# Batch 1's first stage behind batch 0's, the first decodes through PSUM, the last weights decoded earlier

## The chip, the cores and the metric

One core of a Trainium2 chip runs the kernel. The metric is the device time of one execution in microseconds (us), as the median of several. The core has four computing engines with queues of their own: TensorE (PE, with its weight loads as PEld), VectorE (DVE), ScalarE (ACT) and GpSimd (POOL). SyncE (SP) issues most of the DMAs here, and ACT some of the stores. Each queue is worked off in order, so an instruction that waits holds up all that stand behind it on its engine.

## The reference

Three stages follow each other. `x` of one is the result of the one before, 4608 rows of 512.

```
p_packed = softmax(p @ k.T / 8) @ v             # 8 batches x 8 heads, 32 packed rows of 64, 576 keys
out      = softmax(q @ p_packed.T / 8) @ p_packed
x        = out, heads side by side              # 4608 x 512
h = x @ w_in;  x = (h * sigmoid(h)) @ w_out     # 512 -> 2048 -> 512
a = x @ w1;  b = x @ w2                         # 512 -> 1024
out = ((a * b) @ w3) @ w_out2                   # 1024 -> 1024 -> 512
```

The weights come to the chip as 64-bit words and have to be decoded to 32-bit floats there. All products are done in three passes on a high and a low part of each operand (`mm3`: L96, L97, L98).

## The kernel before

**Slots.** The first two stages run as one list of 256 items (8 batches, 2 halves of 288 rows, 16 blocks `m` of 128 hidden columns), called slots here and numbered from 0. A slot has 18 matmuls of 288 columns on PE: six for `ps_h` (the hidden block) and, three slots later (`LAG` = 3), twelve for `ps_x` (its product with `w_out`). Between them stand `sg` (a tanh on ACT), `gg` (DVE, L795), `gh` (ACT) and `gl` (POOL, L89). `ps_h` has two banks, so the `ps_h` of a slot waits for the `gg` of two slots before. The lefthand operand `mq` of a slot is loaded (`mr`, a DMA), rounded by a DVE cast (L84) and completed by a POOL subtraction; two `mr` buffers exist.

**What is woven in.** Beside the slots run units: `Pack` (attention of the packed rows), `Spread` (attention of the queries), and `PackIn` (product of packed values and `w_in`, with `wi` and `ps_m`). Which one is handed out in which slots is set by `over` and `pack_in` (`paces`); a scheduler then orders the instructions of each engine by its own costs. The start is handed out by the string `START`: P0 and P1 are the packs of batches 0 and 1, S0 and S1 the two halves of the queries of batch 0, L a load of an encoded weight, F a decode, D and T products of batch 0 and 1 with `w_in`, W a store of a decoded weight; "|" ends a slot.

**Decoding.** One decode (`Decode`) of a 128x512 block is two operations on ACT (the high and the low words, in place in `raw`), a shift on DVE (L164, `z<-raw`), an addition on POOL (L165, `z<-z,raw`) and a combination on DVE (L166, `z<-raw,z`). The first 32 decodes, of `w_in` and `w_out`, stand in the first 56 slots.

**The last weights.** From slot 209 to slot 250, `prepare_second` prepares the third stage: 40 decodes of `wo2`, `w3`, `w1` and `w2`, the splits `wo`, `w3T`, sums and splits `w12s` on DVE and ACT, and 16 groups of 12 products of 512 columns, `ps_w` (w3 times `wo2`), into one bank, whose splits `w34s` are done by ACT and DVE.

**Third stage.** After slot 255 come 36 items of `ps_ab` and `ps_o` (L1086, L96 to L98), which the change leaves as they are.

Of the kernel before, what the change touches and what calls it, by code (L numbers as in the profile page):

```python
# [22 lines left out]
def attention_swiglu_chain(  # L23
# [109 lines left out]
    w34_d = [dram.tile([128, 2, 512], F32, name=f"w34_d{i}") for i in range(KM2)]  # L133
    x2_d = {(b, f): dram.tile([128, CD, HS], F32, name=f"x2_d{b}_{f}") for b in range(B) for f in range(2)}
# [7 lines left out]
    ps_acc = psum_a.enter_context(tc.tile_pool(name="ps_acc", bufs=4, space=PSUM))  # L142
    ps_h = psum_a.enter_context(tc.tile_pool(name="ps_h", bufs=2, space=PSUM))
    ps_f = psum_a.enter_context(tc.tile_pool(name="ps_f", bufs=2, space=PSUM))

# [4 lines left out]
    class Decode:  # L150
# [7 lines left out]
        def __init__(self, raw, z):  # L158
            def word(dtype, t):
                return raw.bitcast(dtype).rearrange("p (n t) -> p n t", t=2)[:, :, t]  # L160

            act_copy(word(F32, 1), word(F32, 1), 2.0**-112)
            act_copy(word(I32, 0), word(U32, 0), 2.0**-29)
            V.tensor_scalar(out=z, in0=word(I32, 1), scalar1=3, scalar2=None, op0=ALU.logical_shift_left)  # L164
            G.tensor_tensor(out=z, in0=z, in1=word(I32, 0), op=ALU.add)  # L165
            V.scalar_tensor_tensor(  # L166
                out=z, in0=word(I32, 1), scalar=-(2**31), in1=z, op0=ALU.bitwise_and, op1=ALU.bitwise_or
            )
            self.z = z.bitcast(F32)
# [5 lines left out]
    class Decodes:  # L175


        def __init__(self, srcs, finish, raw, room):
            self.srcs, self.finish, self.raw, self.room = srcs, finish, raw, room
            self.n = 0  # L180
            self.end = len(srcs)
            self.raws = []
# [7 lines left out]
        def step(self):  # L190
# [4 lines left out]
            self.finish(n, Decode(self.raws.pop(0), self.room(n)))  # L195
# [42 lines left out]
    class Lane:  # L238
# [99 lines left out]
    class Pack(Rows):  # L338
# [26 lines left out]

        def load_v(self):
            self.v = self.lane.v_rows()
            move(out=self.v, in_=v[self.b, self.hg])

        def split_v(self, f):  # L370
            if self.lane.plain:
                return
            if f == 0:
                self.vp = self.lane.parts([128, 4, 5, 64], "v")
            r, cs = self.PARTS[f]
            hi, lo, src = (x[0:r, :, cs] for x in (*self.vp, self.v))
# [7 lines left out]
        def steps(self):  # L384
# [34 lines left out]
            for c in range(5):  # L419
# [3 lines left out]
                    [x[0:r, c] for x in ep], [x[0:r, :, c] for x in self.vp], c == 0, c == 4,  # L423
# [208 lines left out]
    def direct(g, c):  # L632

        assert all(("i", CD * g + c) in ready for c in range(CD))
# [28 lines left out]
    def finish_fill(n, d):  # L663
# [10 lines left out]
        finish_fill, fill_raw, lambda n: zi[order[n][1]].bitcast(I32) if order[n][0] == "i" else at_room(n),  # L674
    )
# [72 lines left out]
    def fetch(u):  # L748

        while True:  # L750
# [16 lines left out]
            t = g_p.tile([128, 2, 128], F32, tag="mr", name="mr", bufs=2)  # L767
            src = source(b, g, j)
            n = 128 // len(src)
            for y, x in enumerate(src):  # L770
                move(out=t[n * y:n * y + n], in_=x)
            split_hi(slots[:, far, :, 0], t, True)
# [472 lines left out]
```

## Time and profile before

| | us |
|---|---|
| median of 3 runs | 1493.23 (1491.17 to 1495.48) |
| the profiled execution, device time | 1495.0 |
| its span, first to last instruction | 1493.2 |

Busy shares of the span: PE 94%, PEld 88%, DVE 63%, ACT 45%, POOL 40%. The profile's ends of matmuls are modelled, so PE counts as busy between matmuls that follow closely; how fast it really goes is read from how many matmuls stand in a stretch. A share over the whole span is a mean over stretches with different limits: the page's slices show PE below full in the first four and again about half way, where DVE is at nine tenths or more.

### The profile page before, as it was taken

The page shows a single profiled execution, that of the slowest core. Times are in us where ns is not written, and L with a number is a line of the kernel's source. Part 1 is how long each engine was busy: PE and PEld are TensorE (multiplying, and loading weights), DVE is VectorE, ACT ScalarE, POOL GpSimd, SP SyncE. Part 2 cuts the span into 40 slices and gives each one's busy share as a digit, 9 for nine tenths or more (in the row PEclk, how much of TensorE's full clock was granted, in tenths as well). Part 3 has the DMA queues.
Part 4 walks back from the last instruction along what each step waited for, and adds up shares of the span by engine and source line. Part 5 has one row for each costly group of instructions (what it writes and reads, how often), then busy time and mean ns, then how long its engine had stood idle before and what let it go on. Part 6 is the DMA issues. An engine that isn't in the chain of part 4 may idle for free.

```text
span 1493.2 us, 25861 instructions
## 1 busy us (share of the span) xinstructions
PE 1410.7 (94%) x9548; PEld 1318.6 (88%) x9548; DVE 935.8 (63%) x1743; ACT 665.7 (45%) x1442; POOL 596.0 (40%) x606
## 2 busy tenths in 40 slices
PE   6789999999999999999788889999999999999999
PEld 4577899899999999999777779899999999999998
DVE  6977757548674486646999995364553645536443
ACT  5766555645565455644455653132221323213221
POOL 4689645766678456674876552000000000000000
PEclk9989999999999999999999999999999999999999
DMA  7687533754466243542468778810100101101000
GB/s 253 233 295 246 157 96 106 214 147 126 118 184 171 75 121 95 160 112 83 157 216 268 244 238 295 344 57 1 57 29 29 57 1 57 29 29 58 1 29 29
DMA packets 139263, 194.77 MB, mean 130 GB/s; under 512 B 14464, under 2 KB 101504, under 8 KB 138112
## 3 DMA queue, kind: packets, MB, share of 16 engines
q1 hardware_dynamic: 123904, 178.43, 37.4%
q10 hardware_dynamic: 15232, 14.68, 3.0%
q8 instruction: 75, 1.23, 0.3%
q14 instruction: 52, 0.43, 0.1%
HBM read 133.76 MB, written 59.31 MB: 129 GB/s over the span
## 4 chain that ended last, share of the span: by engine, by line
PE 64%; DVE 15%; issue 6%; DMA 6%; ACT 4%; POOL 3%; SPq 1%; ACTq 0%; DVEq 0%; POOLq 0%
PE ps_ab L1086 24%; PE ps_o L96 5%; PE ps_o L97 5%; PE ps_o L98 5%; PE ps_x L96 5%; PE ps_x L98 5%; PE ps_x L97 5%; DMA mr<-m_d 3%; PE ps_h L96 2%; PE ps_h L97 2%; PE ps_h L98 2%; DVE z L166 2%; DVE w12s L89 2%; DVE z L164 1%; DVE mq L84 1%
## 5 line engine op out<-in xcount | busy, mean ns | idle before, releaser
L96 PE MATMUL ps_x<-gh,wo 128*128 128x288 f32 x1024 | 303.7, 300 | 5.0 <-DVE xs L824 2.4
L97 PE MATMUL ps_x<-gh,wo 128*128 128x288 f32 x1024 | 301.4, 298 | 0.0
L98 PE MATMUL ps_x<-gl,wo 128*128 128x288 f32 x1024 | 286.1, 299 | 4.2 <-POOL gl L89 3.9
L89 POOL TENSOR_TENSOR gl<-gg,gh 128x288 fp32r<-128x288 f32 x256 | 226.2, 889 | 106.6 <-ACT gh L80 91.8
L1086 PE MATMUL ps_ab<-xct,w 128*128 128x256 f32 x1728 | 221.4, 284 | 0.0
L1086 PEld LDWEIGHTS ps_ab<-xct,w 128*128 128x128 f32 x1728 | 215.1, 190 | 1.0
L96 PEld LDWEIGHTS ps_x<-gh,wo 128*128 128x128 f32 x1024 | 194.4, 190 | 10.2 <-DVE xs L824 4.1
L80 ACT ACTIVATE gh<-gg 128x288 fp32r<-128x288 f32 x256 | 112.6, 442 | 194.2 <-DVE gg L795 190.7
L97 PEld LDWEIGHTS ps_x<-gh,wo 128*128 128x128 f32 x1024 | 194.3, 190 | 2.2 <-issue 1.3
L98 PEld LDWEIGHTS ps_x<-gl,wo 128*128 128x128 f32 x1024 | 188.1, 190 | 7.4 <-POOL gl L89 5.6
L89 POOL TENSOR_TENSOR mq<-mr,mq 128x256 fp32r<-128x256 f32 x176 | 143.6, 816 | 121.0 <-DVE mq L84 110.0
L96 PE MATMUL ps_h<-a,mq 128*128 128x288 f32 x512 | 159.8, 312 | 33.9 <-DVE gg L795 30.2
L1086 PE MATMUL ps_ab<-xcb,w 128*128 128x256 f32 x1296 | 176.9, 283 | 2.8 <-DMA w<-w_d 2.8
L1103 DVE TENSOR_TENSOR r<-p,ps_ab 128x512 f32<-128x512 f32 x72 | 49.2, 684 | 205.6 <-PE ps_ab L1086 205.4
L1086 PEld LDWEIGHTS ps_ab<-xcb,w 128*128 128x128 f32 x1296 | 168.1, 189 | 7.3 <-issue 2.9
L97 PE MATMUL ps_h<-a,mq 128*128 128x288 f32 x512 | 154.7, 302 | 0.8 <-POOL mq L89 0.8
L98 PE MATMUL ps_h<-a,mq 128*128 128x288 f32 x512 | 153.5, 300 | 0.0
L84 DVE CAST mq<-mr 128x256 fp32r<-128x256 f32 x176 | 85.1, 484 | 103.5 <-PE ps_h L98 52.2
L795 DVE SCALAR_TENSOR_TENSOR gg<-sg,ps_h 128x288 f32<-128x288 f32 x256 | 113.9, 447 | 48.6 <-ACT sg L791 42.2
L96 PEld LDWEIGHTS ps_h<-a,mq 128*128 128x128 f32 x512 | 98.0, 191 | 48.4 <-DVE gg L795 41.6
L791 ACT ACTIVATE sg<-ps_h 128x288 f32<-128x288 f32 x256 | 101.9, 404 | 52.9 <-PE ps_h L98 46.6
L97 PE MATMUL ps_o<-w,abl 128*128 128x512 f32 x280 | 109.7, 392 | 0.0
(165 smaller groups left out, 2619.4 us busy)
## 6 DMA issues: line engine op xcount, KB each, us to landing
mr<-m_d SPq DMA_DIRECT2D x144, 128.0 KB, 2.6
raw<-in_moe_w_dram SPq DMA_DIRECT2D x32, 512.0 KB, 4.3
w_d<-w12s ACTq DMA_DIRECT2D x56, 256.0 KB, 3.0
w<-w_d SPq DMA_DIRECT2D x8, 1792.0 KB, 14.2
wz<-wi_d SPq DMA_DIRECT2D x48, 256.0 KB, 3.4
m_d<-ms SPq DMA_DIRECT2D x96, 128.0 KB, 2.8
raw<-in_moe_w_out_dram SPq DMA_DIRECT2D x21, 512.0 KB, 4.8
vr<-in_v_dram SPq DMA_DIRECT2D x16, 640.0 KB, 4.2
```

The lines of the kernel that those rows point to most:

```text
L80: A.activation(out=dst, in_=src, func=ACTF.Copy, scale=mul)
L84: V.tensor_copy(out=hi, in_=src)
L89: (eng or V).tensor_tensor(out=lo, in0=src, in1=hi.bitcast(F32), op=ALU.subtract)
L96: T.matmul(out=dst, lhsT=wh, rhs=xh, start=start, stop=False)
L97: T.matmul(out=dst, lhsT=wl, rhs=xh, start=False, stop=False)
L98: T.matmul(out=dst, lhsT=wh, rhs=xl, start=False, stop=stop)
L164: V.tensor_scalar(out=z, in0=word(I32, 1), scalar1=3, scalar2=None, op0=ALU.logical_shift_left)
L166: V.scalar_tensor_tensor(out=z, in0=word(I32, 1), scalar=-(2**31), in1=z, op0=ALU.bitwise_and, op1=ALU.bitwise_or)
L791: ins = A.activation(out=sg, in_=ps, func=ACTF.Tanh, scale=0.5)
L795: V.scalar_tensor_tensor(out=gg, in0=sg, scalar=1.0, in1=ps, op0=ALU.add, op1=ALU.mult)
L1086: T.matmul(out=bank[:, x], lhsT=w[:, wp], rhs=xt[:, kt, xp], start=first and (x, kt, n) == (0, 0, 0), stop=last and (x, kt, n) == (1, 1, 2 ...
L1103: V.tensor_tensor(out=dst, in0=p, in1=q, op=op)
```

## The change

1. `START` is written anew: the packs of batch 1 (P1) stand directly behind those of batch 0, before most decodes; S1 comes behind them, and products (T) and stores (W) are spread over more slots. P1 loads its values in pieces into buffers of decoded weights (`vz`).
2. As long as no accumulator of a slot is in use, a decode writes its high words to a PSUM bank (`ps_dec`). The two DVE operations then read PSUM, and POOL's addition comes last instead of between them.
3. The 40 late decodes leave `prepare_second`. They are handed out in slots 70 to 205 (pace "z"), their operations held behind the `sg` of their slot, loads behind an `mr` load; each result is stored to `late_d` in HBM from ACT's queue and is loaded again by `prepare_second` (12 buffers, up to six ahead).
4. `mr` has three buffers, and the split of an `mq` that is not needed in the next slot is handed out one slot after its load, behind a `gg`.

```diff
     START = (
-        "P0.load P0.load_v P0.split_v0 S0.load P0.prepare L L L L P0 F P0 F L P0 F "
...
+        "P0.load P0.load_v P0.split_v0 S0.load P0.prepare L L L P1.load P1.load_v P1.prepare P1.split_v0 L L "
+        "P0 P0 P0 P0 P0.tail S0 S0 P1 F L F L S1.load S0 P1 F L F L D D P1 F L F L P1 F L F L D D P1.tail F "
+        "| F F S1 | F S1 | F F S1 | F F | F F T T | F F T T | F W W | F T T W W | F F T T | W W T T "
...
+    late_d = [dram.tile([128, 512], F32, name=f"late_d{n}") for n in range(5 * KM2)]
...
-        def __init__(self, raw, z):
+        def __init__(self, raw, z, ps=None):
...
-            act_copy(word(F32, 1), word(F32, 1), 2.0**-112)
+            high = word(F32, 1) if ps is None else ps
+            act_copy(high, word(F32, 1), 2.0**-112)
             act_copy(word(I32, 0), word(U32, 0), 2.0**-29)
...
+            high = high.bitcast(I32)
+            V.tensor_scalar(out=z, in0=high, scalar1=3, scalar2=None, op0=ALU.logical_shift_left)
...
+            else:
+
+                V.scalar_tensor_tensor(
+                    out=word(I32, 0), in0=high, scalar=-(2**31), in1=word(I32, 0),
+                    op0=ALU.bitwise_and, op1=ALU.bitwise_or,
+                )
+                G.tensor_tensor(out=z, in0=z, in1=word(I32, 0), op=ALU.add)
...
+        lambda: None if acc else acc_bank(1, "ps_dec"),
...
+        while came and u:
+            with tc.issue_after(behind["gg"]):
+                parts(*came.pop(0))
...
-            t = g_p.tile([128, 2, 128], F32, tag="mr", name="mr", bufs=2)
+            t = g_p.tile([128, 2, 128], F32, tag="mr", name="mr", bufs=3)
...
+                behind["mr"] = move(out=t[n * y:n * y + n], in_=x).ins
+            if nxt > u + 1:
+                came.append((far, t))
+            else:
+                parts(far, t)
...
+        load()
+        load()
+        yield
+        for n in range(len(late)):
+            if n + 2 < len(late):
+                load()
+            with tc.issue_after(behind["sg"]):
+                z = Decode(raws[n], room(n)).z
+            store(out=late_d[n], in_=z, age=1)
+            yield
...
+            def load():
+                n = len(zs)
+                zs.append(dp.tile([128, 512], F32, tag="z", name="z", bufs=12))
+                move(out=zs[n], in_=late_d[n])
...
+    paces["z"].append((70, at0 + 13, len(late) + 1))
```

Here `at0` is 192, so the pace ends at slot 205.

**DVE at slot 228.** Three places show how the instructions move. The first is DVE's queue at slot 228, in the preparation of the third stage, as it was:

```order
L795 SCALAR_TENSOR_TENSOR gg_10629<-sg_10627,ps_h_10608 128x288
L166 SCALAR_TENSOR_TENSOR z_10521<-raw_10519,z_10521 128x512
L795 SCALAR_TENSOR_TENSOR gg_10676<-sg_10674,ps_h_10655 128x288
L164 TENSOR_SCALAR z_10592<-raw_10590 128x512
L89 TENSOR_TENSOR w3T_10694<-z_10521,w3T_10694 128x512
L89 TENSOR_TENSOR w12s_10531<-sums_10472,w12s_10531 128x2x128
L166 SCALAR_TENSOR_TENSOR z_10592<-raw_10590,z_10592 128x512
```

The same place on DVE in the changed kernel, from the `gg` of slot 228 on:

```order
L843 SCALAR_TENSOR_TENSOR gg_10927<-sg_10925,ps_h_10906 128x288
L83 CAST mq_195<-mr_10904 128x2x128
L88 TENSOR_TENSOR w12s_11348<-z_11101,w12s_11348 128x2x128
L948 TENSOR_TENSOR sums_11498<-z_11290,sums_11498 128x256
L88 TENSOR_TENSOR w12s_11354<-z_11101,w12s_11354 128x2x128
L843 SCALAR_TENSOR_TENSOR gg_10968<-sg_10966,ps_h_10947 128x288
L83 CAST mq_195<-mr_10945 128x2x128
```

The two operations of a decode on `z` have gone; the splits and sums stay, and `z` now comes from a load.

**DVE at slot 155.** The second place is DVE's queue at slot 155, in the long middle of the list, before (`sm`, `s2` and `sT` belong to the softmax of a query unit):

```order
L795 SCALAR_TENSOR_TENSOR gg_7611<-sg_7609,ps_h_7590 128x288
L84 CAST mq_155<-mr_7681 128x2x128
L795 SCALAR_TENSOR_TENSOR gg_7654<-sg_7652,ps_h_7633 128x288
L549 TENSOR_SCALAR sm_7193<-sm_7193 128x18
L550 RECIPROCAL sm_7193<-sm_7193 128x18
L551 TENSOR_TENSOR s2_7149<-s2_7149,sm_7193 128x576
```

The same place now (`raw2` and `z2` are those of a late decode):

```order
L843 SCALAR_TENSOR_TENSOR gg_7900<-sg_7898,ps_h_7879 128x288
L83 CAST mq_195<-mr_7877 128x2x128
L173 TENSOR_SCALAR z2_7920<-raw2_7549 128x512
L572 TENSOR_REDUCE mx_7422<-s2_7419 128x18
L88 TENSOR_TENSOR a2_7260<-sT_7315,a2_7260 128x576
L843 SCALAR_TENSOR_TENSOR gg_7951<-sg_7949,ps_h_7930 128x288
L83 CAST mq_195<-mr_7928 128x2x128
L573 TENSOR_TENSOR s2_7419<-s2_7419,mx_7422 128x576
L420 TENSOR_REDUCE mx_7608<-ps_s_7594 128x1
L177 SCALAR_TENSOR_TENSOR z2_7920<-raw2_7549,z2_7920 128x512
```

The two DVE operations of a late decode stand among the `gg` of the slots, with POOL's addition (L176) between them in time.

**SP at the start.** The third place is SP's queue at the start, behind the loads of P0 and S0, in the changed kernel (`raws` and `raw` are encoded weights, `pb`, `rows` and `vz` packed rows, keys and values of P1):

```order
L204 DMA raws<-in_moe_w_in_dram 128x512 x2
L204 DMA raw<-in_moe_w_in_dram 128x512
L105 DMA pb<-in_p_dram 128x256
L105 DMA rows_212<-in_k_dram 128x2x288 x2
L105 DMA pb<-in_p_dram 128x256
L105 DMA rows_213<-in_k_dram 128x2x288 x2
L105 DMA vz<-in_v_dram 128x512 x2
L105 DMA vz<-in_v_dram 128x256
L105 DMA vz<-in_v_dram 128x512 x2
L105 DMA vz<-in_v_dram 128x256
L204 DMA raw<-in_moe_w_in_dram 128x512 x2
```

The same place before, behind the same loads of P0 and S0:

```order
L186 DMA raws<-in_moe_w_in_dram 128x512 x2
L186 DMA raw<-in_moe_w_in_dram 128x512 x3
L106 DMA kq<-in_q_dram 128x2x288
L106 DMA rows_171<-in_q_dram 128x2x288
L106 DMA pr<-in_p_dram 128x256 x2
```

Five loads of encoded weights stood together; now P1's twelve loads stand behind the third.

## Rows read from the trace of the kernel before

**Rows 1.** Six stretches of the span, busy time and instructions of each engine.

```profile
core 0: us, PE busy (x) PEld busy (x) DVE busy (x) ACT busy (x) POOL busy (x), PEclk, DMA share, GB/s
0.00:55.40 55.40, 34.47 (x108) 21.85 (x108) 40.49 (x87) 29.99 (x63) 26.11 (x28) 0.94 0.78 275
55.40:255.20 199.80, 184.61 (x1204) 169.86 (x1205) 144.16 (x298) 117.96 (x278) 139.75 (x135) 0.95 0.56 180
...
314.10:689.20 375.10, 372.52 (x2748) 366.50 (x2747) 240.62 (x551) 206.21 (x486) 245.17 (x271) 1.00 0.43 125
689.20:900.60 211.40, 177.67 (x1083) 160.47 (x1082) 192.47 (x304) 116.58 (x263) 133.40 (x120) 0.96 0.67 213
900.60:1493.30 592.70, 585.23 (x4039) 547.65 (x4037) 286.85 (x453) 160.77 (x279) 7.77 (x9) 0.99 0.19 67
```

**Rows 2.** The same stretches, `gg` alone (L795): one a slot.

```profile
55.40:255.20 199.80, 24.90 (x56) 0.95 0.56 180
314.10:689.20 375.10, 57.19 (x128) 1.00 0.43 125
689.20:900.60 211.40, 21.35 (x49) 0.96 0.67 213
```

**Rows 3.** Waits of PEld, 689.2 to 900.6: total us, times, longest.

```profile
PEld ps_h L96 <- DVE gg L795: 21.9, 19, 2.7
PEld ps_w L96 <- DVE w34s L89: 13.7, 6, 4.5
PEld ps_x L96 <- DVE xs L824: 3.1, 4, 1.7
```

**Rows 4.** Groups, 689.2 to 900.6: busy us, mean ns of one, idle before.

```profile
L165 POOL TENSOR_TENSOR z<-z,raw 128x512 int32<-128x512 int32 x40 | 59.3, 1482 | 37.5 <-ACT raw L80 15.2 <-DVE z L164 7.3 <-ACT sg L791 4.4
L96 PE MATMUL ps_x<-gh,wo 128*128 128x288 f32 x197 | 57.7, 299 | 3.3 <-DVE xs L824 2.2 <-ACT xs L80 1.1
...
L166 DVE SCALAR_TENSOR_TENSOR z<-raw,z 128x512 int32<-128x512 int32 x40 | 36.9, 922 | 0.0
...
L96 PE MATMUL ps_h<-a,mq 128*128 128x288 f32 x98 | 32.1, 328 | 17.0 <-DVE gg L795 17.0
...
L80 ACT ACTIVATE raw<-raw 128x512 f32<-128x512 f32 x40 | 27.1, 677 | 24.1 <-DMA raw<-in_moe_w_dram 4.6 <-DMA raw<-in_moe_w_out_dram 4.6 <-DVE w3T L89 3.0
L96 PE MATMUL ps_w<-wo,w3T 128*128 128x512 f32 x64 | 27.1, 423 | 12.3 <-DVE w34s L89 12.3
...
L164 DVE TENSOR_SCALAR z<-raw 128x512 int32<-128x512 int32 x40 | 24.3, 607 | 4.5 <-ACT raw L80 4.2
```

**Rows 5.** A stretch of 40 us with 288-column matmuls alone.

```profile
480.00:520.00 40.00, 40.00 (x308) 40.00 (x307) 16.92 (x49) 18.99 (x47) 20.14 (x24) 1.00 0.24 76
```

**Rows 6.** The densest sixteen-slot pieces of the middle.

```profile
362.10:405.90 43.80, 43.75 (x334) 43.55 (x334) 36.75 (x90) 25.96 (x63) 28.67 (x33) 1.00 0.46 133
405.90:458.20 52.30, 52.30 (x372) 50.70 (x371) 34.11 (x65) 32.91 (x72) 39.43 (x39) 1.00 0.63 183
...
548.10:594.40 46.30, 45.51 (x342) 44.62 (x341) 36.85 (x88) 25.14 (x64) 29.94 (x35) 1.00 0.36 107
```

**Rows 7.** Waits of PEld, 314.1 to 689.2.

```profile
PEld ps_h L96 <- DVE gg L795: 2.6, 3, 1.9
```

**Rows 8.** DVE lines, whole span: shortest, median and longest ns.

```profile
L166 DVE SCALAR_TENSOR_TENSOR z<-raw,z x53: 672/681/1800, 41.9 to 892.1; 128x512 int32<-128x512 int32 x53
...
L1103 DVE TENSOR_TENSOR r<-p,ps_ab x72: 679/682/689, 927.1 to 1477.8; 128x512 f32<-128x512 f32 x72
```

**Rows 9.** DVE decode groups before slot 0, 0 to 55.4.

```profile
L166 DVE SCALAR_TENSOR_TENSOR zi<-raws,zi 128x512 int32<-128x512 int32 x4 | 4.9, 1221 | 0.0
...
L164 DVE TENSOR_SCALAR z<-raw 128x512 int32<-128x512 int32 x2 | 0.8, 408 | 0.0
```

**Rows 10.** Stretches of the start.

```profile
10.00:20.00 10.00, 7.22 (x37) 5.67 (x36) 4.75 (x21) 7.62 (x22) 1.27 (x1) 1.00 1.04 401
20.00:30.00 10.00, 5.49 (x20) 3.20 (x19) 9.14 (x19) 7.64 (x16) 6.34 (x5) 1.00 0.62 204
30.00:40.00 10.00, 6.81 (x14) 3.05 (x13) 9.97 (x18) 5.05 (x10) 5.37 (x5) 0.83 0.36 128
```

**Rows 11.** The chain of waits at the start: start us, us, what.

```profile
3.76 0.61 SPq L106
...
8.41 6.32 DMA raws<-in_moe_w_in_dram
```

More of the change, by code (lines that the diff above doesn't have):

```diff
@@ L364, in prepare @@
                 split(*self.pb, self.p)
+        v_in_pieces = False
         def load_v(self):
-            self.v = self.lane.v_rows()
-            move(out=self.v, in_=v[self.b, self.hg])
+            src = v[self.b, self.hg]
+            if self.v_in_pieces:
+                self.v = []
+                for c in range(0, 5, 2):
+                    n = min(2, 5 - c)
+                    t = at.tile([128, 512], F32, tag="z", name="vz", bufs=NZ)
+                    t = t.rearrange("p (c h d) -> p c h d", c=2, h=4)
+                    move(out=t[:, 0:n], in_=src[:, c:c + n])
+                    self.v += [t[:, y] for y in range(n)]
+            else:
+                self.v = self.lane.v_rows()
+                move(out=self.v, in_=src)
         def split_v(self, f):
@@ L632, in direct @@
     def direct(g, c):
-        assert all(("i", CD * g + c) in ready for c in range(CD))
+        assert ("i", CD * g + c) in ready
         ps = bank("ps_m0")
@@ L748, in fetch, with parts @@
     def fetch(u):
+        def parts(far, t):
+            split_hi(slots[:, far, :, 0], t, True)
+            split_lo(slots[:, far, :, 1], t, slots[:, far, :, 0], G)
+        while came and u:
+            with tc.issue_after(behind["gg"]):
+                parts(*came.pop(0))
         while True:
@@ L770, in fetch @@
             for y, x in enumerate(src):
-                move(out=t[n * y:n * y + n], in_=x)
-            split_hi(slots[:, far, :, 0], t, True)
-            split_lo(slots[:, far, :, 1], t, slots[:, far, :, 0], G)
+                behind["mr"] = move(out=t[n * y:n * y + n], in_=x).ins
+            if nxt > u + 1:
+                came.append((far, t))
+            else:
+                parts(far, t)
+    came = []
     gt = {}
@@ L827, in emit_x2, with decode_late, raw, room @@
             move(out=x2_d[b, f], in_=xs)
+    late, late_srcs = [], []
+    for j in range(KM2):
+        late.append(("o", j))
+        late_srcs.append(wo2[128 * j:128 * j + 128, :])
+    for n in range(2 * KM2):
+        late.append(("3", n))
+        late_srcs.append(w3[n])
+        half, x, kt, y = n // 8, n // 4 % 2, n // 2 % 2, n % 2
+        c = kt + 2 * y
+        late.append(("12", n))
+        late_srcs.append((w1, w2)[x][128 * c:128 * c + 128, 512 * half:512 * half + 512])
+    def decode_late():
+        def raw():
+            return at.tile([128, 512], U64, tag="raw2", name="raw2", bufs=3)
+        def room(n):
+            return at.tile([128, 512], I32, tag="z2", name="z2", bufs=2)
+        raws = []
+        def load():
+            raws.append(raw())
+            with tc.issue_after(behind["mr"]):
+                DMA.dma_start(out=raws[-1], in_=late_srcs[len(raws) - 1])
+        load()
[8 more added lines that the diff above has]
+            yield
     def prepare_second():
@@ L923, in prepare_second @@
                 for _ in range(2):
-                    if dec.n < dec.end:
-                        dec.step()
+                    if used[0] < len(late):
+                        step()
                     some(3)
@@ L1030, in all_steps @@
         yield from prepare_second()
-    streams = {"x": all_steps(), "y": chain(ins)}
-    done = {"x": 0, "y": 0}
+    streams = {"x": all_steps(), "y": chain(ins), "z": decode_late()}
+    done = {"x": 0, "y": 0, "z": 0}
     for i, (b, f, m) in enumerate(items):
         if i == KM:
-            behind.clear()
+            for eng in (DMA, A):
+                behind.pop(eng, None)
         flush()
```

88 lines of the change are left out of this document (43 added, 45 removed), and 5 rows, old and new, of the table START.

## The prediction

> **What bounds the kernel now.** I read the six stretches first [rows 1]. The reader is to see that PE is the limit in the middle (372.5 us busy of 375.1, clock 1.00) and in the third stage (585.2 of 592.7), but not in two places: up to slot 56, at 255.2 us, and from 689.2 to 900.6 us. The count of `gg` [rows 2] turns stretches into slots: 128 slots in the middle take 375.1 us, 2.9 each; the 49 of the late stretch take 211.4, 4.3 each. In the late stretch DVE is the full engine, 192.5 of 211.4 us (91%), while PE has 177.7.
>
> Then the waits of the late stretch [rows 3]: PE's weight loads stand 21.9 us for `gg`, 13.7 for the split of `ps_w` and 3.1 for the eviction of `ps_x`, all three from DVE, 38.7 us together. In the middle the largest such wait is 2.6 us in all [rows 7]. So DVE's work before slot 209 is nearly free, and after it is paid for in span.
>
> **Late stretch: the decodes go.** The groups [rows 4] give 40 shifts of 607 ns (24.3 us) and 40 combinations of 922 ns (36.9 us) on DVE: 61.2 us leave. What stays on DVE is 192.5 - 61.2 = 131.3 us, far under the 211.4. POOL loses 59.3 us, ACT 40 pairs at 677 ns, 54 us; these were not the limit. DVE loses its place as the limit, and PE is next. Its need comes from two sides. By waits: 211.4 - 38.7 = 172.7. By counts: 308 matmuls of 288 columns fill 40.00 us [rows 5], 130 ns each; the stretch has 197 + 196 + 196 for `ps_x` and 3 x 98 for `ps_h` (three lines each, of which one stands in [rows 4]), 883 x 0.130 = 114.8 us, and 3 x 64 of `ps_w` at 512 columns, 0.130 x 512/288 = 0.231 us, 44.4 us: 159.2 in all. The gain lies between 38.7 and 52.2 if DVE's waits all go, and above nothing if `ps_w`'s single bank or the remaining splits hold PE. I take 39: the waits are measured, while the count supposes PE without a gap. What is late next is `ps_w` against its own split `w34s`.
>
> What replaces the decode is a load of 256 KB from `late_d`, up to six ahead; SP's queue loses 40 loads of 512 KB in this stretch, so the DMA share (0.67) falls. These loads stand ahead of `mr` loads on SP, as the larger ones did.
>
> **Middle: the decodes come.** The same work lands in 375.1 us. By the same durations DVE goes from 240.6 to 301.8 us (80%), POOL from 245.2 to 304.5 (81%), ACT from 206.2 to 260 (69%), and DMA from 125 GB/s by 40 x (0.52 + 0.26) MB / 375.1 us = 84 to about 209 GB/s, where the start has moved 401 [rows 10]. On the mean PE covers all of it: 375.1 us of PE against at most 304.5. The cover is thin in pieces [rows 6]. Spread evenly, 61.2 us of DVE give 7.1 us to the piece of 43.8 (36.75 + 7.1 = 43.9, all of it), 7.6 to that of 46.3 (44.4, 96%), and 59.3 of POOL give 8.3 to that of 52.3 (47.7, 91%). Behind a late DVE operation wait the `gg` of the slot (and so `ps_h` two slots on), behind POOL's addition the `gl`, behind ACT's store to `late_d` (which waits for the combination) the `sg`, behind SP's load of an encoded block the `mr`. Three slots of lag and, for `mr`, a third buffer and a later split stand against that.
>
> The two ends: at best nothing is lost and the 2.6 us of waits go too, -3. At worst DVE time is paid one for one, as where it is full: +61. The nearest rows are the late stretch, where a DVE at 91% goes with 38.7 of 211.4 us of waits (18%), and the first piece of [rows 6], where a DVE at 84% costs PE nothing (43.75 of 43.8 busy). The three thin pieces are 142 us; 18% of them would be 26. Since the cost must begin between 84 and 91%, and the rest of the middle is below that, I take +10.
>
> A sentence on why late decodes may slow each other: the combination on `z` takes 672 ns at its shortest and 1800 at its longest, while an operation of the same width with an operand in PSUM keeps to 679 to 689 [rows 8]. The Trainium skill, "SBUF — State Buffer", section "Who interferes with whom", says that a DVE instruction with two SBUF inputs and a GpSimd instruction that reads SBUF exclude each other for the whole instruction, and one with at most one SBUF input does not take part. The rows agree. The late decodes keep the SBUF form (the accumulators are in use by then), so by that rule they would be worth more than their 61.2 us where POOL is busier; this is the mechanism behind the slower rival below.
>
> **Start: decodes through PSUM, P1 early.** DVE is full from 20 us on [rows 10]. The twelve decodes before slot 0 took 20.6 us of DVE (eight groups, of which [rows 9] show the first and the last), 1.72 each; with PSUM operands I take twice L1103's 684 ns [rows 8], 1.37. Fourteen decodes have the new form in the built order: 14 x 0.35 = 4.9 us less. P1's DVE operations only move from behind slot 0 to before it, inside the same stretch to 255.2 us, where DVE's total falls by those 4.9. The other end is SP: P1's twelve loads stand ahead of the fourth encoded block, 12 x 0.6 us [rows 11] = 7.2 us, at a time when DMA is full (1.04, 401 GB/s, [rows 10]). I expect P0's, S0's and P1's own operations to fill DVE meanwhile; if not, +7. If also POOL is freed and the `mr` waits between 100 and 200 us shrink, -10. I take -4.
>
> **Third stage.** The matmuls behind slot 255 are the same and in the same order: 0.
>
> **Sum.** The span of 1493.2 - 4 + 10 - 39 = 1460.2, with the 1.8 us around it (1495.0 - 1493.2) 1462. The median of the runs is 1.8 below the profiled execution, so 1460.
>
> **The rivals.** *The toll eats the gain (slower).* Late decodes in SBUF form make DVE and POOL hold each other, and each decode's 1.53 us of DVE is paid in PE time: +61 - 39 - 4 = +18, 1511. For it: [rows 8], the piece that goes to 100%, and the late stretch, where this is so. Against it: in [rows 7] PE hardly waits at a mean DVE load of 64%, and 80% is below the 84% that cost nothing. It decides from 43/40 = 1.1 us of PE a decode on. Chance 0.13.
>
> *The late stretch is held by something else.* `ps_w` has one bank, and its 16 groups still need the split between them; if those 13.7 us stay and half of the waits for `gg`, the stretch gains 14: -4 + 10 - 14 = -8, 1485. For it: six waits of up to 4.5 us [rows 3]. Against: `w34s` waits on DVE's queue, which gets short. Chance 0.15.
>
> *All goes well.* Window 52, middle 0, start -10: -62, 1431. For it: PE's need by counts. Against: no stretch with `ps_w` has run without gaps. Chance 0.14.
>
> That the change doesn't do what it says I leave out: in the built order the decodes stand in slots 70 to 205.
>
> **How the numbers follow.** The forecast has 0.58, with a range of its own of 1442 to 1478. A difference of 0.3%, 4.5 us, is about what a measurement of this kernel can tell from no change. The forecast and the good case are faster, 0.72; of the second rival, whose 1485 is close to the bound of 1488.7, 0.10 is faster and 0.05 the same; of the slower rival 0.10 is slower and 0.03, with a toll near 1.1 us, the same. So 0.82, 0.08, 0.10. The range of 1434 to 1488 leaves out the slower rival and the lower half of the good case, about 0.2.
>
> **What would show it.** Right: from slot 200 to slot 248 about 172 us instead of 211, DVE busy there near 131 us, the waits for `gg` below 10; the middle's 128 slots in 380 to 390 us, with DVE and POOL near 80%, and the added waits of PE in the pieces that [rows 6] show; slot 0 at 50 to 56 us, shifts and combinations with PSUM operands near 684 ns without long ones. Wrong: waits of PE for `gg` or `gl` of tens of us in the middle, combinations of the late decodes with a median far above 681 ns (the slower rival), or waits for `w34s` as long as before (the second).

## The result and the profile after

The changed kernel took 1476.12 us in the median (1475.26 to 1476.68), the kernel before beside it 1494.36; the ratio is 0.9879, 95% interval 0.9858 to 0.9899. The forecast was 1460 with a range of 1434 to 1488: faster, as expected, by 18 us instead of 33. The profiled execution took 1475.26 us.

These are the windows of the changed kernel, cut at the same slots as [rows 1] (slot 0, 56, 72, 200, 248 by the starts of `gg`, now L843); the third row is the stretch that [rows 1] leaves out.

```profile
0.00:51.90 51.90, 37.43 (x134) 25.25 (x134) 35.60 (x100) 32.99 (x77) 18.47 (x24) 0.97 0.78 272
51.90:240.40 188.50, 172.55 (x1145) 157.83 (x1146) 141.63 (x271) 112.49 (x257) 141.50 (x138) 0.96 0.61 193
240.40:313.80 73.40, 64.40 (x411) 59.06 (x411) 42.98 (x82) 40.82 (x89) 47.78 (x49) 0.93 0.63 181
313.80:715.40 401.60, 383.69 (x2760) 371.65 (x2760) 310.87 (x616) 239.33 (x555) 313.67 (x307) 0.99 0.62 192
715.40:878.60 163.20, 158.27 (x1036) 147.35 (x1035) 107.54 (x224) 75.66 (x186) 71.89 (x83) 1.00 0.66 217
878.60:1473.50 594.90, 588.21 (x4070) 551.28 (x4068) 287.43 (x453) 161.27 (x279) 7.71 (x9) 1.00 0.18 66
```

| stretch | before | after | difference | forecast |
|---|---|---|---|---|
| to slot 0 | 55.4 | 51.9 | -3.5 | -4, with the next row |
| slots 0 to 56 | 199.8 | 188.5 | -11.3 | |
| slots 56 to 72 | 58.9 | 73.4 | +14.5 | no term |
| slots 72 to 200 | 375.1 | 401.6 | +26.5 | +10 |
| slots 200 to 248 | 211.4 | 163.2 | -48.2 | -39 |
| slot 248 to the end | 592.7 | 594.9 | +2.2 | 0 |

So the late stretch gave more than expected, the middle took more, and the start's 14.8 us were gone again at slot 72 (314.1 before, 313.8 after).

The waits of PE's weight loads in the late stretch (total us, times, longest), which answer to [rows 3]:

```profile
PEld ps_h L95 <- DVE gg L843: 3.9, 6, 1.2
PEld ps_w L95 <- DVE w34s L88: 2.9, 3, 1.4
```

Of 38.7 us 6.8 are left on these lines, and PE is busy 97% of the stretch. DVE fell to 107.5 us, not to 131.3, because what stayed there got shorter. Two groups of DVE in the late stretch, the first fence from before, the second from after (busy us, mean ns of one, idle before):

```profile
L84 DVE CAST mq<-mr 128x256 fp32r<-128x256 f32 x32 | 19.3, 604 | 0.0
...
L89 DVE TENSOR_TENSOR w3T<-z,w3T 128x512 fp32r<-128x512 f32 x16 | 17.0, 1064 | 2.1 <-ACT w3T L80 2.0
```

```profile
L83 DVE CAST mq<-mr 128x256 fp32r<-128x256 f32 x32 | 12.5, 390 | 0.0
L88 DVE TENSOR_TENSOR w3T<-z,w3T 128x512 fp32r<-128x512 f32 x16 | 11.5, 718 | 8.2 <-ACT w3T L79 8.0
```

Part of the 48.2 us is a shift across the cut at slot 248. Of the 64 `ps_w` products a pass ([rows 4]), 60 stand in the stretch now; one of the 16 groups comes behind it:

```profile
L95 PE MATMUL ps_w<-wo,w3T 128*128 128x512 f32 x60 | 23.8, 396 | 2.2 <-DVE w34s L88 2.0
```

In the middle it is the other way round. The waits for `gg` of PE's products and of its weight loads, slots 72 to 200; the second line answers to the 2.6 us of [rows 7]. Both stand for the same `gg`, so they are not added:

```profile
PE ps_h L95 <- DVE gg L843: 14.7, 12, 3.6
...
PEld ps_h L95 <- DVE gg L843: 19.3, 18, 3.8
```

The middle's groups of the decode on DVE and POOL, and the cast of `mq` beside them:

```profile
L83 DVE CAST mq<-mr 128x256 fp32r<-128x256 f32 x97 | 50.8, 523 | 7.8 <-DMA mr<-m_d 6.0 <-PE ps_x L97 1.5
L177 DVE SCALAR_TENSOR_TENSOR z<-raw,z 128x512 int32<-128x512 int32 x39 | 44.1, 1130 | 17.9 <-POOL z L176 17.6
...
L173 DVE TENSOR_SCALAR z<-raw 128x512 int32<-128x512 int32 x39 | 23.1, 593 | 0.1
```

```profile
L176 POOL TENSOR_TENSOR z<-z,raw 128x512 int32<-128x512 int32 x39 | 55.3, 1418 | 15.0 <-ACT raw L79 6.5 <-ACT gh L79 4.8 <-DVE z L173 2.7
```

A decode keeps DVE busy for 1.72 us there, and DVE stands 17.6 us more behind POOL's addition. That gave three theories for the middle: DVE's queue standing at that addition (Q), the length of operations with two SBUF operands (P), the bare work on DVE and POOL (W); and, beside the engines, the loads (M) and ScalarE's copies (S).

Slots 56 to 72 have waits for loads of batch 2's `m`. DVE's waits there, then those of SP's queue:

```profile
DVE mq L83 <- DMA mr<-m_d: 15.5, 6, 5.0
```

```profile
SPq L105 <- POOL v L88: 8.6, 1, 8.6
SPq L105 <- DVE x L88: 7.5, 1, 7.5
```

SP stands for buffers of the units' values and keys, and loads that come later in its queue start later. That this is what holds slots 56 to 72 is argued, not shown; e6 comes back to it.

### The profile page after: what moved, and what is told of

Same layout as the page of the kernel before. It is cut to its first block, busy times and chain, and to the rows that moved or that the text cites. A ratio compares the mean times of both kernels' runs of the same rounds, so it can differ in the third digit from the quotient of the medians.

```text
span 1473.5 us, 26073 instructions
## 1 busy us (share of the span) xinstructions
PE 1404.5 (95%) x9548; PEld 1312.4 (89%) x9548; DVE 926.1 (63%) x1743; ACT 662.6 (45%) x1442; POOL 601.0 (41%) x606
## 5 line engine op out<-in xcount | busy, mean ns | idle before, releaser
L88 POOL TENSOR_TENSOR gl<-gg,gh 128x288 fp32r<-128x288 f32 x256 | 232.0, 908 | 94.8 <-ACT gh L79 85.9
L88 POOL TENSOR_TENSOR mq<-mr,mq 128x256 fp32r<-128x256 f32 x176 | 148.9, 847 | 133.5 <-DVE mq L83 68.5
L843 DVE SCALAR_TENSOR_TENSOR gg<-sg,ps_h 128x288 f32<-128x288 f32 x256 | 114.0, 446 | 82.4 <-ACT sg L838 37.0
L97 PE MATMUL ps_o<-w,abh 128*128 128x512 f32 x280 | 109.6, 391 | 0.0
## 6 DMA issues: line engine op xcount, KB each, us to landing
w<-w_d SPq DMA_DIRECT2D x8, 1792.0 KB, 14.8
```

Of the source, the lines that this page charges most:

```text
L88: (eng or V).tensor_tensor(out=lo, in0=src, in1=hi.bitcast(F32), op=ALU.subtract)
L97: T.matmul(out=dst, lhsT=wh, rhs=xl, start=False, stop=stop)
L843: ins = V.scalar_tensor_tensor(out=gg, in0=sg, scalar=1.0, in1=ps, op0=ALU.add, op1=ALU.mult)
```

## The experiments

All were timed beside the kernel before (1492.0 to 1493.1 in these comparisons) and are edits of the changed kernel. Stretches are cut at the same slots. How far the middle varies with nothing changed in it shows in the changed kernel, e2, e3 and e6: 401.6, 402.2, 405.6 and 402.1 us, one profiled execution each.

**e1: the late decodes go back to `prepare_second`.**

```diff
-                step()
+                dec.step()
...
-    paces["z"].append((70, at0 + 13, len(late) + 1))
```

> The late decodes stand in the preparation of the third stage again, in slots 209 to 250; all else is as changed. Theory 1 (the late decodes alone make the difference from slot 72 on): slots 72 to 200 go back from 401.6 to about 375 us, slots 200 to 248 from 163.2 to about 211, so the total is 1476 - 27 + 48 = 1497, within 6 us of the kernel before. Theory 2 (the late decodes, whose first loads and operations start in slot 70, also cost the 14.5 us that slots 56 to 72 lost): that stretch goes back from 73.4 to 59 us as well, total about 1483.

1487.78 us, ratio 0.996 (0.9945 to 0.9974). Windows of the middle and of the late stretch:

```profile
312.30:683.90 371.60, 370.77 (x2744) 366.08 (x2743) 228.58 (x537) 202.74 (x477) 238.62 (x270) 1.00 0.42 124
683.90:893.90 210.00, 180.51 (x1080) 165.99 (x1079) 193.47 (x304) 115.45 (x263) 135.38 (x121) 0.93 0.65 214
```

So 40 late decodes cost the middle 30.0 us (0.75 each in the mean) and the late stretch 46.8 (1.17 each). The difference is 16.8 us, but the spans of the two kernels (1486.1 and 1473.5) differ by 12.6 only: in the changed kernel the part behind slot 248 is 2.7 us longer, partly by the shifted `ps_w` group, and slot 72 comes 1.5 later. Theory 2 falls, since slots 56 to 72 take 70.5 us here too. The middle is 3.5 us shorter than in the kernel before, inside the spread named above.

**e2: the old `START` string.**

```diff
-        "P0.load P0.load_v P0.split_v0 S0.load P0.prepare L L L P1.load P1.load_v P1.prepare P1.split_v0 L L "
...
+        "P0.load P0.load_v P0.split_v0 S0.load P0.prepare L L L L P0 F P0 F L P0 F "
...
```

> Only the hand-written order of the start is the old one. Theory 1 (what the start gains by slot 56 is lost by slot 72, because the units of batches 2 and 3 set the time of slots 56 to 72 whatever the start does): slot 56 comes at about 255 us instead of 240, slots 56 to 72 take about 59 instead of 73, and the total stays within 4 us of 1476. Theory 2 (the new order is worth its 15 us, and the loss at slots 56 to 72 has another cause): total about 1490.

1473.63 us, ratio 0.9878 (0.9847 to 0.9908): the same as with the new string. Windows of slots 0 to 56 and 56 to 72:

```profile
47.90:258.40 210.50, 187.00 (x1228) 170.19 (x1227) 156.49 (x308) 126.36 (x290) 146.18 (x140) 0.97 0.56 180
258.40:312.80 54.40, 51.17 (x349) 48.08 (x348) 26.53 (x49) 29.25 (x65) 42.66 (x45) 1.00 0.78 233
```

Slot 56 comes 18 us later than with the new string, slot 72 one us earlier. To slot 0 the old string is the faster one, by 4.0 us.

**e3: first decodes without PSUM.**

```diff
-        lambda: None if acc else acc_bank(1, "ps_dec"),
+        lambda: None,
```

> The first fourteen decodes write their high words in place in SBUF again, POOL's addition stands between the two operations on DVE; the order of the start is the new one. If the PSUM form is worth what its durations say, slot 0 comes 14 x 0.35 = 5 us later at most, and by Theory 1 the total stays within 4 us of 1476, since slot 72 does not move. If the start's 15 us come from the PSUM form and reach the end, total about 1490.

1478.57 us, ratio 0.9906 (0.9878 to 0.9935). Slot 0 comes at 60.6 instead of 51.9 us, and again slot 72 at 314.2:

```profile
0.00:60.60 60.60, 40.23 (x140) 28.02 (x140) 42.26 (x110) 37.75 (x85) 23.98 (x28) 0.88 0.69 241
```

So the PSUM form is worth 8.7 us at slot 0, more than the 5 expected, and next to nothing at slot 72.

**e4: no late decodes in slots 86 to 106 and 150 to 170, two of the dense pieces of [rows 6].**

```diff
-    paces["z"].append((70, at0 + 13, len(late) + 1))
+    for lo, hi, n in ((70, 86, 8), (106, 150, 20), (170, at0 + 13, len(late) - 27)):
+        paces["z"].append((lo, hi, n))
```

> The same 41 steps of the late decodes, but none in slots 86 to 106 and 150 to 170, where the loss of 7.4 + 9.6 of 26.5 us lies; they stand closer in slots 70 to 86, 106 to 150 and 170 to 205. Theory A (a local overload: softmax operations and decodes together exceed PE's time there): the two pieces go back to about 44 and 46 us, the others gain a few, slots 72 to 200 take 384 to 392 instead of 401.6, total 1459 to 1468. Theory B (each late decode costs PE about 0.66 us wherever it stands, by holding queues or the port): slots 72 to 200 stay at 400, total 1473 to 1480.

1482.89 us, ratio 0.9935 (0.992 to 0.995). Slots 88 to 104, 104 to 120, 120 to 136 and 168 to 200, then the middle and the late stretch:

```profile
368.20:412.70 44.50, 43.99 (x335) 43.62 (x335) 32.37 (x83) 25.57 (x66) 33.03 (x36) 1.00 0.42 132
412.70:467.70 55.00, 53.84 (x364) 50.38 (x363) 45.72 (x75) 37.66 (x82) 44.89 (x41) 1.00 0.77 242
467.70:523.70 56.00, 50.20 (x352) 47.94 (x351) 46.65 (x88) 33.65 (x81) 49.84 (x48) 0.97 0.75 240
620.10:712.70 92.60, 90.64 (x643) 87.29 (x643) 69.68 (x115) 57.24 (x129) 78.14 (x78) 1.00 0.67 208
313.10:712.70 399.60, 383.04 (x2751) 370.74 (x2750) 317.15 (x615) 238.24 (x555) 310.32 (x307) 0.99 0.61 193
712.70:884.90 172.20, 161.56 (x1043) 149.51 (x1043) 109.57 (x226) 73.58 (x185) 72.57 (x84) 0.99 0.63 206
```

The spared piece is free (44.5), the next two pay 7.9 and 13.9 us against e1's 47.1 and 42.1, and the sum stays: 28.0 us above e1 instead of 30.0. So sparing the dense pieces gains nothing. But a decode has no fixed price: the 14 in slots 104 to 136 pay 21.8 us, the 11 in slots 168 to 200 nothing (92.6 us against e1's 94.9). Why the late stretch lost 9 us here is not settled; the waits of PE's weight loads for `w34s` there doubled to 5.9 us.

**e8: POOL's addition last, still in SBUF.**

```diff
-            if ps is None:
+            if ps is None and not last:
...
-                z = Decode(raws[n], room(n)).z
+                z = Decode(raws[n], room(n), last=True).z
```

> Late decodes stay in SBUF, but VectorE combines sign and low word before GpSimd's addition, which comes last (the order that the PSUM form has). In the changed kernel VectorE stands 17.6 us in the middle (slots 72 to 200) for GpSimd's addition of the 39 decodes there, and the gg of a slot stands behind it. Theory Q (VectorE's queue standing at the addition makes gg late): PE's waits for gg in the middle fall from 34 us by about half, the middle from 402 to 384 to 392 us, the total to 1460 to 1468. Theory P (what counts is the length of operations with two SBUF operands, 1130 ns instead of 680, and what they add to their neighbours): the order changes nothing, middle 398 to 405, total 1474 to 1480. Theory W (what counts is the bare sum of work on VectorE and GpSimd, 77 and 78 % of the middle): the same as P here, and e5 tells P from W.

1476.18 us, ratio 0.9879 (0.9859 to 0.9899); the middle 405.4 us. DVE no longer waits for the addition, and the waits for `gg` fall from 14.7 to 10.7 us (products) and from 19.3 to 14.1 (weight loads; the 34 us of the expectation add the two), but no time comes back:

```profile
PE ps_h L95 <- DVE gg L843: 10.7, 10, 2.9
...
PEld ps_h L95 <- DVE gg L843: 14.1, 13, 3.1
```

Theory Q falls: DVE standing at that addition is not what the middle pays.

**e5: the late decodes through PSUM.**

```diff
-                z = Decode(raws[n], room(n)).z
+                z = Decode(raws[n], room(n), bank("ps_dec")).z
```

> Late decodes get the PSUM form: the high word goes through a PSUM bank of the shared pair, and the addition comes last. Theory P: VectorE's combination falls from 1130 to about 700 ns, 39 x 0.43 = 17 us of VectorE less in the middle, the splits near them get shorter (cast of mq 523 to about 450 ns), the middle 380 to 390 us, total 1455 to 1465, clearly under e8. Theory Q: as e8, since the order is the same, within 3 us of it. Theory W: both stay near the changed kernel, middle 395 to 405. A cost on the other side: the pair of banks serves the units too, so TensorE may wait for a bank; then waits of ps_s or ps_o on ACT or VectorE appear and eat up to 10 us.

1474.75 us, ratio 0.9875 (0.9856 to 0.9894). The middle's window, and in it DVE's groups of the decode and of the `mq` cast:

```profile
311.60:711.30 399.70, 384.34 (x2760) 373.12 (x2759) 298.40 (x616) 243.56 (x555) 289.17 (x308) 0.99 0.62 194
```

```profile
L83 DVE CAST mq<-mr 128x256 fp32r<-128x256 f32 x97 | 61.0, 629 | 17.8 <-DMA mr<-m_d 16.1 <-PE ps_x L97 1.4
...
L173 DVE TENSOR_SCALAR z<-ps_dec 128x512 int32<-128x512 int32 x39 | 26.7, 684 | 9.1 <-ACT ps_dec L79 7.1 <-DMA late_d<-z 2.0
L182 DVE SCALAR_TENSOR_TENSOR raw<-ps_dec,raw 128x512 int32<-128x512 int32 x39 | 26.5, 680 | 0.1
```

The combination falls from 1130 to 680 ns, as P expected, and the middle stays: the cast of `mq` rose from 523 to 629 ns (97 x 0.106 = 10 us), so DVE is only 12.5 us lighter, and 12.5 us of DVE and 24.5 of POOL less go with a gain of 1.9 us, inside the spread. As stated, P falls: its 380 to 390 us didn't come. But e5 does not take away what neighbours cost each other: part of it moved to the casts, and DVE stands 16.1 us for `mr` loads instead of 6.0. The late stretch took 170.6 us here, 7 more than in the changed kernel; this was not followed up.

What holds a cast shows in the changed kernel's middle. A cast and the POOL operation during which it began (start, length in us):

```profile
352.56 1.37 DVE L83 CAST mq<-mr 128x256 fp32r<-128x256 f32 x1
```

```profile
352.47 1.30 POOL L176 TENSOR_TENSOR z<-z,raw 128x512 int32<-128x512 int32 x1
```

The shortest cast of the stretch took 0.27 us; this one ended 0.16 us after POOL's addition. All 32 casts of 0.6 us or more there began during a POOL operation and ended 0.14 to 0.16 us after it. In e5 there are 40 of that length.

**e9: loads and stores alone.**

```diff
+        zero = at.tile([128, 512], F32, tag="z2", name="z2", bufs=2)
+        G.memset(zero, 0.0)
...
-            with tc.issue_after(behind["sg"]):
-                z = Decode(raws[n], room(n)).z
-            store(out=late_d[n], in_=z, age=1)
+            store(out=late_d[n], in_=zero, age=1)
```

> The late decodes do no engine work: their blocks are still loaded and 256 KB each still stored, but from a tile of zeros (this leaves the decoding of the late weights out; what follows slot 209 works on zeros, so only the stretches to slot 200 are read). With all decodes moved back the middle took 371.6 us, with the late decodes in it 401.6: 30 us for 40 decodes, and neither GpSimd's place in the order (405.4) nor the PSUM form (399.7) changed it. Theory M (the added 67 GB/s and SP's queue delay the loads of m and keys): middle 385 to 400. Theory W (engine work alone): middle 371 to 377.

1481.22 us, ratio 0.9935 (0.9918 to 0.9951). The windows to slot 0 and of the middle:

```profile
0.00:76.40 76.40, 46.19 (x132) 28.59 (x132) 33.01 (x99) 28.58 (x67) 14.24 (x22) 0.78 0.85 308
346.00:717.50 371.50, 370.69 (x2742) 365.79 (x2742) 231.23 (x537) 202.15 (x477) 238.25 (x270) 1.00 0.59 181
```

The middle costs nothing more than e1's. It carries the 40 loads only: a store that waits for no decode went out at once, all 40 stand before slot 0, and the start pays 24.5 us. The next run has both in their places.

**e10: loads, stores and ScalarE's two copies.**

```diff
-                z = Decode(raws[n], room(n)).z
-            store(out=late_d[n], in_=z, age=1)
+                w = raws[n].rearrange("p n -> p n")
+                for t, d, s, k in ((1, F32, F32, 2.0**-112), (0, I32, U32, 2.0**-29)):
+                    act_copy(*(w.bitcast(x).rearrange("p (n t) -> p n t", t=2)[:, :, t] for x in (d, s)), k)
+            store(out=late_d[n], in_=raws[n].bitcast(F32)[:, 0:512], age=1)
```

> The late decodes keep their loads, stores and the two scaling copies on ScalarE, and leave out what VectorE and GpSimd do (so the late weights are not decoded; only the stretches to slot 200 are read). Theory S (ScalarE's two copies of 0.68 us stand ahead of the tanh and of the copy gh, and so make gg late): most of the 30 us stays, middle 390 to 400. Theory W (VectorE and GpSimd): middle 371 to 380. A split of the two is open: then in between, and the next run has the rest.

1450.15 us, ratio 0.9725 (0.970 to 0.975).

```profile
312.40:685.60 373.20, 371.86 (x2750) 366.75 (x2749) 229.64 (x539) 243.62 (x555) 237.62 (x269) 1.00 0.66 208
```

At 208 GB/s, and with 41 us more of ACT than in e1, the middle takes 1.6 us more. M and S fall; what costs is what DVE and POOL do for a decode, together with what then waits for it. ACT's queue is part of that: its store of a block stands for DVE's combination, and in the changed kernel's middle ACT waits 8.7 us there.

**e11: the operations of DVE and POOL without ScalarE's copies.**

```diff
-            act_copy(high, word(F32, 1), 2.0**-112)
-            act_copy(word(I32, 0), word(U32, 0), 2.0**-29)
+            if copies:
+                act_copy(high, word(F32, 1), 2.0**-112)
+                act_copy(word(I32, 0), word(U32, 0), 2.0**-29)
...
-                z = Decode(raws[n], room(n)).z
+                z = Decode(raws[n], room(n), copies=False).z
```

> The late decodes keep their loads, stores and the operations of VectorE and GpSimd, and leave out the two copies on ScalarE (so the late weights are not the right ones; only the stretches to slot 200 are read). Theory W: most of the 30 us stays, middle 390 to 402. Theory S: middle 371 to 382. If e10 and this one are both under 380, the cost is neither alone but the chain over all three engines in a slot.

1497.9 us, ratio 1.0047 (1.0028 to 1.0067): slower than the kernel before. Window of the middle, and DVE's longest wait in it:

```profile
313.20:741.40 428.20, 394.90 (x2742) 381.47 (x2741) 314.32 (x617) 198.68 (x477) 307.04 (x307) 0.96 0.58 180
```

```profile
DVE z L174 <- DMA raw<-in_moe_w_dram: 34.4, 16, 3.3
```

The cost stays, as W says, and 26.6 us come on top that no theory had: without the copies DVE stands 34.4 us for the load of `raw`, with the `gg` behind it. In the changed kernel ScalarE reads these loads first, and stands only 0.1 us there (its copy of the high words, middle; the last number is the idle time before it):

```profile
L79 ACT ACTIVATE raw<-raw 128x512 f32<-128x512 f32 x39 | 26.3, 675 | 0.1
```

So the wait was not handed from ScalarE to DVE; it is new in e11, and why DVE comes to the loads too early there is not shown. e11 doesn't give the price of DVE and POOL by itself; e10 does, as the difference to the changed kernel: 401.6 - 373.2 = 28.4 us.

**e7: two `mr` buffers, no deferred split (part 4 of the change undone).**

```diff
-            t = g_p.tile([128, 2, 128], F32, tag="mr", name="mr", bufs=3)
+            t = g_p.tile([128, 2, 128], F32, tag="mr", name="mr", bufs=2)
...
-            if nxt > u + 1:
-                came.append((far, t))
-            else:
-                parts(far, t)
+            parts(far, t)
```

> Without the third buffer of mr and the deferred split, the rest as changed. Theory 1 (this part only keeps the late decodes from holding up slots): the middle gets longer by 5 to 15 us, PE waits for mq or mr appear there, total 1478 to 1490; slots 56 to 72 the same, 70 to 75. Theory 2 (the deferral itself delays splits of mr behind gg, and so costs slots): the middle the same or shorter, 395 to 402 us, slots 56 to 72 shorter by up to 10, total 1464 to 1476.

1492.09 us, ratio 0.9992 (0.9981 to 1.0003): no gain is left. Windows of slots 0 to 56, 56 to 72 and 72 to 200, and DVE's longest wait in the last:

```profile
51.10:252.30 201.20, 177.60 (x1172) 161.52 (x1173) 146.84 (x286) 115.03 (x263) 144.85 (x141) 0.97 0.57 184
252.30:309.70 57.40, 55.72 (x375) 52.21 (x375) 31.61 (x55) 33.96 (x74) 44.30 (x44) 1.00 0.72 208
309.70:732.80 423.10, 393.59 (x2770) 378.94 (x2769) 322.13 (x631) 243.10 (x563) 312.60 (x309) 0.98 0.59 184
```

```profile
DVE mq L83 <- DMA mr<-m_d: 37.2, 28, 4.3
```

Theory 1 is right on the middle, beyond its upper end: it is 21.5 us longer, DVE standing 37.2 us for `mr` instead of 6.0. On slots 56 to 72 it missed: they take 57.4 us, not 70 to 75. The buffer and the deferred split went together, so which of them counts is open. It is also this part, not the new `START` alone, that made slots 0 to 56 faster (201.2 without it), and there its gain is given back by slot 72.

**e6: units of batches 1 to 3 handed out 3 to 6 slots earlier.**

```diff
-    over(15, 20, plain([Spread(1, 0), Spread(1, 1)]))
-    over(26, 38, [Pack(2, 0, 0), Pack(2, 1, 0), Pack(3, 0, 1), Pack(3, 1, 1)])
-    pack_in(44, 66, [2, 3])
-    over(44, 62, [Spread(2, 0), Spread(2, 1)])
+    over(12, 17, plain([Spread(1, 0), Spread(1, 1)]))
+    over(20, 32, [Pack(2, 0, 0), Pack(2, 1, 0), Pack(3, 0, 1), Pack(3, 1, 1)])
+    pack_in(38, 60, [2, 3])
+    over(38, 56, [Spread(2, 0), Spread(2, 1)])
```

> The units of batches 1 to 3 in the slots before 62 are handed out 3 to 6 slots earlier, the rest as changed. In the changed kernel slot 56 comes 14.8 us earlier than before and slot 72 at the same time: slots 56 to 72 take 73.4 instead of 58.9 us, with 15.5 us of waits for loads of batch 2's m. Theory U (batch 2's units are handed out too late in time now that the slots run earlier): slots 56 to 72 fall to 58 to 64 us, slot 72 comes at 300 to 306 instead of 314, total 1461 to 1468. Theory V (the work and loads of slots 0 to 72 together set slot 72, wherever the units stand): slots 0 to 56 get longer by what 56 to 72 get shorter, slot 72 stays at 311 to 317 us, total 1472 to 1478.

1467.02 us, ratio 0.9827 (0.9806 to 0.9847), the fastest of those that decode all weights. Slots 0 to 56 and 56 to 72:

```profile
50.60:248.90 198.30, 179.26 (x1189) 166.46 (x1190) 146.22 (x290) 117.82 (x267) 146.70 (x141) 0.95 0.58 188
248.90:303.60 54.70, 53.41 (x364) 50.54 (x364) 27.41 (x55) 31.81 (x70) 45.11 (x46) 1.00 0.82 250
```

Slot 72 comes at 303.6 instead of 313.8, and the 10 us reach the end. U is right on the total; V had a part of it, since slots 0 to 56 got 9.8 us longer. DVE's waits for `mr` in slots 56 to 72 did not fall, they are 19.6 us here against 15.5; SP's longest wait there fell from 8.6 to 3.2 us. So the early units are shown to bring slot 72 forward, the way by which they do it is not.

**e12: e6, and 16 of the 40 late decodes back in the late stretch.**

```diff
+    back = [n for n in range(len(late)) if n % 5 in (1, 3)]
...
+                if n in back:
+                    z = Decode(z, dp.tile([128, 512], I32, tag="zb", name="zb", bufs=3)).z
```

> The earlier units of e6, and 16 of the 40 late decodes, spread evenly, go back to the late stretch; 24 stay in slots 70 to 205. What e9 to e11 showed: loads and ScalarE's copies cost the middle nothing (371.5 and 373.2 us), so its 30 us are VectorE's and GpSimd's work, 0.75 us a decode, and with the decodes packed denser in places it stayed 0.72. So the middle should give back 16 x 0.75 = 12 us against e6 (402.2 to about 390). Theory L (the late stretch's price is as even, 47 us for 40 decodes, 1.17 each): it rises by 19 us, from 163 to 182, total 1471 to 1477, slower than e6's 1467. Theory R (the late stretch has room: VectorE 107 of 163 us, GpSimd 72, TensorE 158 of 163, so the first decodes cost it little): it rises by 0 to 6 us, total 1455 to 1462, the fastest of all.

1469.61 us, ratio 0.9851 (0.9835 to 0.9868): not faster than e6. Middle and late stretch:

```profile
302.90:688.50 385.60, 377.22 (x2760) 369.79 (x2759) 283.13 (x594) 229.06 (x534) 280.11 (x291) 1.00 0.53 166
688.50:871.80 183.30, 164.55 (x1052) 152.52 (x1051) 141.92 (x256) 90.96 (x215) 97.32 (x99) 0.97 0.65 215
```

The middle gives 16.5 us instead of the 12 expected, 1.03 a decode; the 24 that stay cost 14.0 over e1's 371.6, 0.58 each. So in the middle the price of a decode rises with their number. The late stretch takes 20.5 us (1.28 each). Theory L is right: there is no free room in the late stretch either, although DVE's share there is only 77%.

## Why the prediction was half right

*Late stretch, -39.* Right in mechanism, low in size: 48.2. Some 6 us of that, by an estimate, are matmuls which now stand behind slot 248: by the prediction's rates the need of the matmuls in the stretch fell from 159.2 us to 152.9 (568 for `ps_x`, 288 for `ps_h`, 180 of `ps_w`), and PE took 10.3 us more than that. With the 2.2 us lost behind the cut 46.0 remain, between the prediction's two sizes, 38.7 by the waits and 52.2 by the counts. The DVE term of 131.3 us failed because it kept the old durations of the splits, which were longer with the decodes beside them. The second rival is out: the waits of PE's weight loads for `w34s` fell from 13.7 to 2.9 us.

*Middle, +10.* This step failed: "Since the cost must begin between 84 and 91%, and the rest of the middle is below that". The mean shares came out near the worked ones (DVE 77%, POOL 78%), and yet the decodes cost 30.0 us against e1, with PE's weight loads waiting 19.3 us for `gg`. Where these 30.0 us lie shows in pieces of sixteen slots. The three thin pieces of [rows 6] lost 4.0, 7.0 and 10.1 us, 21.1 together; the other five lost 8.9, of which slots 72 to 88 4.8. So the alternative that I had worked out and not taken, 26 us in the three thin pieces, had most of the place right and was near in size. What failed is the threshold: at much the same DVE share slots 72 to 88 (74%) lost 4.8 us and slots 184 to 200 (75%) nothing. Slots 120 to 136 of the changed kernel, where five decodes cost 0.3 us although POOL is at 96%, and 152 to 168, where five cost 10.1 us:

```profile
471.40:513.80 42.40, 41.65 (x302) 40.33 (x301) 24.73 (x45) 22.26 (x52) 40.67 (x44) 1.00 0.73 231
562.40:618.30 55.90, 49.70 (x359) 47.17 (x358) 51.69 (x103) 32.76 (x77) 39.03 (x40) 1.00 0.54 166
```

e4 shows that emptying the thin pieces only moves the loss. e9 and e10 put it on what DVE and POOL do for a decode and on what waits for that, 0.75 us of PE a decode in the mean. How it divides between the two engines, and between their work and their holding each other up, was not separated. Of the signs that I had set for the slower rival the median of the combination, far above 681 ns, did appear, and waits for `gg` of 19.3 us, at a price below the 1.1 us at which it decides. The lines of the combination, shortest, median and longest ns, in the changed kernel, which answer to [rows 8] (SBUF form, then PSUM form):

```profile
L177 DVE SCALAR_TENSOR_TENSOR z<-raw,z x49: 680/1277/1785, 72.1 to 720.7; 128x512 int32<-128x512 int32 x49
```

```profile
L182 DVE SCALAR_TENSOR_TENSOR raw<-ps_dec,raw x8: 654/679/692, 21.9 to 61.2; 128x512 int32<-128x512 int32 x8
```

The second line shows the PSUM form free of long ones. What the Trainium skill, "SBUF — State Buffer", section "Who interferes with whom", says of operations with two SBUF inputs agrees with it. The prediction left out a condition of that section, which excepts operations with one SBUF input only outside DVE's two-port modes. The rows of e5's section show that a one-input operation does take part here: the cast of `mq` ends with POOL's operation; in which mode it runs no run shows. By the rule on two inputs alone e5 should have given back up to the 17.6 us that the combinations lost (39 x 0.45). It gave 1.9, so the toll on the combinations isn't by itself what the middle pays. The toll on the casts grew in e5, and no run takes both away: that DVE and POOL holding each other up makes a good part of the 30 us stays possible.

*The cover of `mr`.* The prediction named the third buffer only as something that stands against waits. e7 shows it, with the later split, to be worth 16 us of the total, nearly the whole gain of 18. Without it the whole change gains nothing.

*Start, -4.* Slot 0 came 3.5 us earlier, with PSUM operations at the length assumed. That the size fits is luck: e3 puts the PSUM form at 8.7 us, where 4.9 were counted, and e2 the new order at 4.0 the other way. And the term was to reach the end, but none of this does: with slot 0 at 47.9 (e2), 51.9 and 60.6 us (e3), slot 72 comes at 312.8, 313.8 and 314.2. This holds only so far: in e9, with slot 0 at 76.4, slot 72 comes at 346.0. I gave slots 56 to 72 no term and never looked at what holds them. e6 shows that units of batches 1 to 3, handed out by slot number, move slot 72 when they come earlier.

*Third stage, 0.* Behind slot 248 it took 2.2 us more; 592 to 597 us in all these runs. The `ps_w` group that now stands there, 12 products of 0.231 us by the prediction's rate, is 2.8 us, about as much; in e1, where all groups stand before the cut, the part behind it takes 592.2 us.

*The sum.* -0.3 at slot 72, +26.5, -48.2 and +2.2 make -19.8, by the spans -19.7. The errors of the middle (+16.5) and of the late stretch (-9.2) partly cancel. By e1 the move of the decodes makes 12.6 of it: 16.8 in the two stretches, less what slot 72 and the part behind slot 248 lose.

## What to carry to other kernels

Price a moved piece of work at both places by a run that has it at neither and one that has it at each: here a decode cost 1.2 us where it was and 0.75 where it went, both as means. Such a mean is no fixed price: in the middle 24 decodes cost 0.58 each and the next 16 1.03. An engine's mean share over a long stretch says little about what more work on it costs when its queue also carries a short operation that each step waits for; look at it piece by piece, and let a run, not a share, name the price. And a gain at the start counts only up to the next point whose work is handed out by position; look for that point before counting it.

## What the runs showed of the hardware

The same DVE cast of 128x256 took 390 ns in the mean in the late stretch after, 430 in the middle before, 523 in the middle after and 629 in e5: what runs beside it sets it as much as its size. When it began during an operation of POOL it could last to 0.14 to 0.16 us after that operation's end, though it has only one input in SBUF; in e5, where the combinations got shorter, more casts did so. And a wait of DVE for a DMA is paid by its whole queue: in e11 DVE stood 34.4 us for loads, and the middle was 26.6 us longer than in the changed kernel, though 41 us of ScalarE's work (239.3 - 198.7) had gone.
